# Moving the score-difference matmul from a three-bank to a four-bank PSUM ring in a two-attention, gated prompt kernel

## The chip, the cores and the metric

The kernel runs on one core of a Trainium2 chip. The metric is the device time of one execution in microseconds (us). A core has a matrix engine (PE, with its weight loads shown apart as PEld), a vector engine (DVE), a scalar engine (ACT), GpSimd (POOL) and an engine that here only issues DMAs (SP). Matmuls write into PSUM, which has eight banks of 128 partitions by 512 fp32 values. Every engine takes its own instructions in program order, and engines wait for one another through semaphores.

## The reference: what is computed

Two attention blocks read the same `x` (2048 tokens, 512 wide) with separate weights, each with 32 heads of width 16. Their results are mixed with a gate per token:

```python
q, k, v = split(x @ wqkv)                      # per block, 32 heads of 16
p = softmax(q @ k.T * 16 ** -0.5)              # full, 2048 x 2048 per head
a = (p @ v) @ wo                               # the same for b with its own weights
g = sigmoid((x * gate_w).sum(-1))
out = g * a + (1 - g) * b
```

The 64 heads (32 in each block) give 64 score matrices of 2048 by 2048.

## The kernel before: tiles, stages and order

**Stages.** A prologue (to about 300 us) projects `x` onto queries, keys and values and writes them to DRAM by head. The main stage (about 305 to 2841 us) goes through the 64 heads, 16 key tiles of 128 keys each. The last 75 us finish the last head and the output projection. Output projections of finished groups of heads (`project_out`, L449 to L464) also stand inside the main stage, 16 at about 1659 us and 16 at about 2644 us.

**Two sets of scores.** Softmax needs the maximum of each query's row ahead of the exponentials. So the scores are computed twice. Plain scores (a query tile of 128 rows against 512 keys, L135) are only reduced to a row maximum; they run 20 tiles ahead. Transposed scores (128 keys against 512 queries, L615) carry the maxima in two added rows, go through `exp` on ACT (L617) into the tile `p`, and `p` is multiplied with `v` into the bank `acc` (L576).

**Plain scores by differences.** A query tile needs the maximum over four blocks of 512 keys. On every second tile, blocks 0 and 1 are taken together: one matmul gives the score *differences* (`x_st` holds key block 1 minus key block 0; `max_rise`, L144), ACT takes their positive part, `relu` (L147), into a buffer `rise` in SBUF, and DVE adds that to the scores of block 0 and takes the maximum in one instruction (`max_pair`, L149 to L153). So one DVE pass covers two blocks.

**The round.** The loop at L626 takes two key tiles at a time; I call one pass a round. Its order is written out by hand in a string, read letter by letter (L640):

```python
    FULL = "m3memeem3meAe2Dmeee"
```

Here `m` is a plain score block with its DVE maximum (L145), `e` a transposed score block with its exp (L642), `D` the differences with their relu (L648), `A` the block that is added to them (L651), and a digit so many quarters of the product with `v` (L661). I number the letters: m1 to m6, e1 to e8. A round therefore issues on PE: m1, 3 quarters, m2, e1, m3, e2, e3, m4, 3 quarters, m5, e4, A, e5, 2 quarters, D, m6, e6, e7, e8. ACT has nine passes in a round (e1 to e5, D, e6 to e8), DVE seven (m1 to m5, A, m6). The pair A in a round uses the differences that D wrote in the round before.

**Two matmuls at a time.** Score matmuls use 48 or 50 of the array's 128 rows. `rows()` (L117) lets them alternate between the lower and the upper half, so that two neighbours can run side by side. Products with `v` use all rows, in four column groups.

**PSUM.** Three banks are the ring `ps_m` (L61), four the ring `ps_st` (L327), one is `acc`. A tile of a ring takes the banks in turn: with three banks a matmul waits until the engine that reads the tile three before it is done, with four banks the tile four before it. In the round, `ps_m` serves m1 to m6, A and D, eight tiles; `ps_st` serves e1 to e8. A `project_out` takes one more tile of `ps_m` (L445).

**Once a head** (every eighth round): ACT copies `acc` out (`ev`, L593) between e5 and D, DVE reduces the maxima (`mrow`, L161) at the end of a round and transposes them (`mt`, L168) in another.

Of the kernel before, what the change touches and what calls it, by code (L numbers as in the profile page):

```python
# [23 lines left out]
F32 = mybir.dt.float32  # L24
# [8 lines left out]
P = 128  # L33
# [18 lines left out]
def gated_mha(ctx: ExitStack, tc: tile.TileContext, xT, x, wqkv_a, wo_a, wqkv_b, wo_b, gate_w, out):  # L52
# [8 lines left out]
    ps_m = ctx.enter_context(tc.tile_pool(name="ps_m", bufs=3, space=PSUM))  # L61
# [55 lines left out]
    def rows():  # L117
        turn[0] ^= 1
        return HALVES[1 - turn[0]]

    def scores_bank(m, c):
        h, t = divmod(m, NT)
        if h not in mxp:
            mxp[h] = small.tile([P, NT, 4], F32, name="mxp")
            if h:
                pool.memset(mxp[h][:, FIRST % NT if h == 1 else 0::2, 1:2], LOWEST)
        ps = ps_m.tile([P, 512], F32, name="ps_m")
        b = rows()
        q = q_st[h % 3]
        if c == "rise":  # L130
            assert b == 0
            k = x_st[h % 2][:]
        else:
            k = k_st[h % 3][b:b + SC, c * 512:(c + 1) * 512]
        pe.matmul(ps, q[b:b + SC, t * P:(t + 1) * P], k, start=True, stop=True)  # L135
        return ps, mxp[h][:, t]

    def max_plain(m, c):
        ps, o = scores_bank(m, c)
        dve.tensor_reduce(o[:, c:c + 1], ps, op=ALU.max, axis=AX.X)  # L140
# [3 lines left out]
    def max_rise(m):  # L144
        ps, _ = scores_bank(m, "rise")  # L145
        rises[m] = small.tile([P, 512], F32, name="rise")
        act.activation(rises[m], ps, AF.Relu)  # L147

    def max_pair(m):  # L149
        ps, o = scores_bank(m, 0)  # L150
        rise = rises.pop(m)
        dve.tensor_tensor_reduce(out=rise, in0=ps, in1=rise, scale=1.0, scalar=LOWEST,  # L152
                                 op0=ALU.add, op1=ALU.max, accum_out=o[:, 0:1])  # L153
# [173 lines left out]
    ps_st = ctx.enter_context(tc.tile_pool(name="ps_st", bufs=4, space=PSUM))  # L327
# [369 lines left out]
```

## Time and profile before

| What | Value |
|---|---|
| Median of three runs | 2918.81 us (2918.76 to 2918.82) |
| The profiled execution, own time | 2918.34 us |
| Its span in the profile | 2916.6 us |
| Granted PE clock, mean | 0.998 |
| Relu passes of differences (L147) | 501 |
| exp passes (L617) | 4096 |

The span is what the profile covers; 1.7 us of the execution's own time lie around it. Busy time is the time in which an engine had at least one instruction running. The PE's busy time has modelled ends and says little about waits: where the PE waits, its matmuls in flight still count. The weight loads (PEld) show when the PE issued, and in brackets how long the weight path was idle and what ended that; a gap while a long product streams is no stall.

### The profile page before, as it was taken

How to read it: one execution, taken by the hardware profiler on the slowest of the kernel's cores; microseconds unless marked ns; L12 is line 12 of the kernel's file. 1: busy time of each engine (PE TensorE's matmuls, PEld its weight loads, DVE VectorE, ACT ScalarE, POOL GpSimd, SP SyncE). 2: the span in 40 equal slices, each digit the busy share in tenths (PEclk: the TensorE clock that was granted, in tenths of full speed). 3: DMA queues.
4: the chain of work that ended last, by engine and by line, in shares of the span. 5: the costliest groups of instructions: out<-in, count | busy, mean ns of one | idle time of the engine just before them, and what ended most of it. 6: DMA issues, size and time to landing. Idle time of an engine off the chain costs nothing.

```text
span 2916.6 us, 65382 instructions
## 1 busy us (share of the span) xinstructions
PE 2898.3 (99%) x26176; PEld 1417.1 (49%) x26176; DVE 2392.9 (82%) x4399; ACT 2497.8 (86%) x4758; POOL 255.0 (9%) x456
## 2 busy tenths in 40 slices
PE   8999999999999999999999999999999999999999
PEld 6877444444444444444444455444444444444544
DVE  4145899999899999999999877899999899998784
ACT  3221899999999999999999877899999999998785
POOL 1010112100000000000100231000000001011201
PEclk9999999999999999999999999999999999999999
DMA  7673333223333322333432342332223333233302
GB/s 258 193 255 129 78 70 77 60 53 55 67 60 57 57 57 46 54 57 56 86 56 52 93 103 54 56 58 49 58 50 57 56 75 67 52 70 87 70 13 90
DMA packets 91126, 225.25 MB, mean 77 GB/s; under 512 B 24150, under 2 KB 34358, under 8 KB 78278
## 3 DMA queue, kind: packets, MB, share of 16 engines
q1 hardware_dynamic: 88262, 212.15, 32.5%
q0 software_dynamic: 2560, 8.91, 1.2%
q8 instruction: 206, 3.38, 0.5%
q14 instruction: 98, 0.80, 0.1%
HBM read 152.07 MB, written 68.94 MB: 76 GB/s over the span
## 4 chain that ended last, share of the span: by engine, by line
PE 97%; DMA 1%; ACT 1%; DVE 0%; issue 0%; SPq 0%; DVEq 0%
PE ps_m L135 39%; PE acc L576 37%; PE ps_st L615 10%; PE ps_pro L232 5%; PE ps_m L458 3%; PE ps_pro L264 3%; ACT p L617 1%; DMA raw<-in_xT 0%; DMA k_st<-kd 0%; DMA qd<-part 0%; PE ps_st L458 0%; PE ps_st L509 0%; DVE mxp L140 0%; PE ps_m L509 0%; DVE part L237 0%
## 5 line engine op out<-in xcount | busy, mean ns | idle before, releaser
L617 ACT ACTIVATE p<-ps_st 128x512 f32<-128x512 f32 x4096 | 2153.7, 606 | 118.0 <-PE ps_st L615 84.5
L140 DVE TENSOR_REDUCE mxp<-ps_m 128x1 f32<-128x512 f32 x3094 | 1956.7, 684 | 261.1 <-PE ps_st L615 190.7
L135 PE MATMUL ps_m<-k_st,q_st 48*128 48x512 f32 x3595 | 1375.2, 453 | 0.9 <-DVE mxp L140 0.4
L576 PE MATMUL acc<-p,vg 128*17 128x384 f32 (+1 forms) x16368 | 1186.2, 384 | 2.9 <-ACT ev L584 2.0
L615 PE MATMUL ps_st<-q_st,k_st 50*128 50x512 f32 x4096 | 1187.4, 421 | 0.0
L135 PEld LDWEIGHTS ps_m<-k_st,q_st 48*128 48x128 f32 x3595 | 616.1, 184 | 690.3 <-ACT p L617 298.2
L615 PEld LDWEIGHTS ps_st<-q_st,k_st 50*128 50x128 f32 x4096 | 606.1, 185 | 45.8 <-ACT p L617 24.4
L576 PEld LDWEIGHTS acc<-p,vg 128*17 128x17 f32 x16368 | 314.8, 96 | 455.2 <-issue 435.6
L152 DVE CUSTOM_DVE_ANT_0 rise<-ps_m,rise 128x512 f32<-128x512 f32 x501 | 339.9, 678 | 0.0
L147 ACT ACTIVATE rise<-ps_m 128x512 f32<-128x512 f32 x501 | 301.5, 602 | 42.4 <-PE ps_m L135 0.3
L135 PE MATMUL ps_m<-x_st,q_st 48*128 48x512 f32 x501 | 249.4, 498 | 0.0
L162 POOL CAST mparts<-mrow 128x16 fp32r<-128x16 f32 x64 | 12.7, 198 | 2119.3 <-DVE mrow L161 2119.3
L135 PEld LDWEIGHTS ps_m<-x_st,q_st 48*128 48x128 f32 x501 | 91.7, 183 | 212.3 <-DVE mxp L140 183.8
L236 ACT CAST part<-ps_pro 128x1024 fp32r<-128x1024 f32 x32 | 32.5, 1015 | 134.8 <-PE ps_pro L232 113.3
L237 DVE TENSOR_TENSOR part<-ps_pro,part 128x1024 fp32r<-128x1024 f32 x32 | 39.2, 1224 | 101.1 <-ACT part L236 81.7
L458 PE MATMUL ps_m<-wo,ot 128*128 128x512 f32 (+1 forms) x354 | 90.7, 401 | 0.1
L267 ACT COPY v_st<-ps_pro 128x512 f32<-128x512 f32 x31 | 18.2, 587 | 77.8 <-PE ps_pro L264 74.6
L232 PE MATMUL ps_pro<-xh,whi 128*128 128x512 f32 x256 | 72.5, 402 | 9.6 <-ACT xh L218 9.1
L458 PEld LDWEIGHTS ps_m<-wo,ot 128*128 128x128 f32 (+1 forms) x354 | 64.0, 188 | 20.6 <-ACT rise L147 5.8
L232 PE MATMUL ps_pro<-xh,wlo 128*128 128x512 f32 x256 | 69.4, 393 | 0.0
L232 PE MATMUL ps_pro<-xl,whi 128*128 128x512 f32 x256 | 69.0, 391 | 0.0
L232 PEld LDWEIGHTS ps_pro<-xh,whi 128*128 128x128 f32 x256 | 47.3, 189 | 25.4 <-ACT xh L218 11.8
(99 smaller groups left out, 807.1 us busy)
## 6 DMA issues: line engine op xcount, KB each, us to landing
k_st<-kd SPq DMA_DIRECT2D x128, 256.0 KB
q_st<-qd SPq DMA_DIRECT2D x128, 256.0 KB
qd<-part SPq DMA_DIRECT2D x32, 512.0 KB
kd<-part SPq DMA_DIRECT2D x32, 512.0 KB
k_st<-kd SPq DMA_DIRECT2D x128, 128.0 KB
q_st<-qd SPq DMA_DIRECT2D x128, 128.0 KB
od<-ev SPq DMA_DIRECT2D x63, 256.0 KB
vd<-v_st SPq DMA_DIRECT2D x32, 272.0 KB
```

The source lines that it names most:

```text
L135: pe.matmul(ps, q[b:b + SC, t * P:(t + 1) * P], k, start=True, stop=True)
L140: dve.tensor_reduce(o[:, c:c + 1], ps, op=ALU.max, axis=AX.X)
L147: act.activation(rises[m], ps, AF.Relu)
L152: dve.tensor_tensor_reduce(out=rise, in0=ps, in1=rise, scale=1.0, scalar=LOWEST, op0=ALU.add, op1=ALU.max, accum_out=o[:, 0:1])
L232: pe.matmul(ps[:, c * 512:(c + 1) * 512], a[:, k], b[:, k], start=n == 0, stop=n == 3 * KC - 1)
L236: act.copy(pt[0], ps)
L237: dve.tensor_tensor(pt[1], ps, pt[0].bitcast(F32), op=ALU.subtract)
L264: pe.matmul(ps[:, :DM], a[:, k, o:o + P], b[:, k], start=n == 0, stop=n == 3 * KC - 1)
L458: pe.matmul(ps, ot[a][:n, slot, sl], wt[b][:n, g], start=G == groups[0] and i == 0, stop=G == groups[-1] and i == 2)
L576: pe.matmul(acc[32 * c:32 * c + 17, qa * P:qb * P], v[:, 4 * a + c if final else kt, j], p[:, c * 512 + qa * P:c * 512 + qb * P], start=fi ...
L615: pe.matmul(ps, k[b:b + SC + 2, kk * P:(kk + 1) * P], q[b:b + SC + 2, cc * 512:(cc + 1) * 512], start=True, stop=True)
L617: act.activation(pt[r][:, c * 512:(c + 1) * 512], ps, AF.Exp, scale=SCALE)
```

## The change

The matmul of the score differences takes its PSUM tile from the ring `ps_st` in place of `ps_m`. Relu then reads a bank of `ps_st`. Nothing else in the source changes; `ps_m` serves seven tiles a round and `ps_st` nine.

```diff
-        ps = ps_m.tile([P, 512], F32, name="ps_m")
+        pool_ = ps_st if c == "rise" else ps_m
+        ps = pool_.tile([P, 512], F32, name="ps_st" if c == "rise" else "ps_m")
         b = rows()
         q = q_st[h % 3]
         if c == "rise":
```

The line numbers after it are one higher than in the kernel before.

## The prediction

> **What bounds the kernel now.** I read the windows of the main stage first, then one round instruction by instruction, then the waits. The busy times in a window (PE, PEld, DVE, ACT, POOL; then the clock), and the same window with the difference matmuls alone:
>
> ```profile
> 1000.00:1200.00 200.00, 200.00 (x1970) 89.01 (x1966) 180.76 (x339) 194.36 (x375) 5.45 (x19) 1.00 0.30 57
> ```
>
> ```profile
> 1000.00:1200.00 200.00, 20.39 (x41) 1.00 0.30 57
> ```
>
> 41 rounds in 200 us make a round of 4.88 us. ACT looks full at 194 of 200 us, but its passes overlap, so busy time hides how much more it could do. The timeline of one round tells that; letters are those of the round's string (D is the matmul from `x_st`):
>
> ```profile
> 1016.60 0.68 DVE L140 TENSOR_REDUCE mxp<-ps_m 128x1 f32<-128x512 f32 x1
> ...
> 1017.16 0.49 PE L135 MATMUL ps_m<-x_st,q_st 48*128 48x512 f32 x1
> ...
> 1017.33 0.50 PE L135 MATMUL ps_m<-k_st,q_st 48*128 48x512 f32 x1
> ...
> 1017.80 0.08 DVE L152 DVE_READ_ACCUMULATOR2_ANT mxp<- 128x1 f32 x1
> 1017.86 1.30 DVE L140 TENSOR_REDUCE mxp<-ps_m 128x1 f32<-128x512 f32 x2
> 1017.93 0.18 PEld L135 LDWEIGHTS ps_m<-k_st,q_st 48*128 48x128 f32 x1 [0.25 <-DVE mxp L152]
> ...
> 1019.13 0.50 PE L135 MATMUL ps_m<-k_st,q_st 48*128 48x512 f32 x1
> ...
> 1019.67 2.48 DVE L140 TENSOR_REDUCE mxp<-ps_m 128x1 f32<-128x512 f32 x4 [0.50 <-PE ps_st L615]
> ...
> 1022.03 0.50 PE L135 MATMUL ps_m<-x_st,q_st 48*128 48x512 f32 x1
> ```
>
> D to D is 1022.03 - 1017.16 = 4.87 us. DVE stood idle 0.50 us before m2, so it isn't the bound. Two matmuls are late. m6 (1017.33) could run beside D but starts 0.17 later: it takes the bank of m5, whose maximum ends at 1016.60 + 0.68 = 1017.28; the PE goes on 0.05 later. m1 of the next round (1017.93) takes A's bank, and A's last DVE instruction ends at 1017.80 + 0.08 = 1017.88, again 0.05 before. So the PE waits for the three-bank ring, at a place where DVE is still working through m5, A and m6 one after the other. In the waits view (sum, times, longest):
>
> ```profile
> PEld ps_m L135 <- DVE mxp L152: 126.5, 490, 0.3
> ```
>
> That is m1's alone. What both waits cost is seen in a round of this same trace that began with empty rings, because the PE had just run at half clock and both readers had caught up:
>
> ```profile
> 313.54 0.50 PE L135 MATMUL ps_m<-x_st,q_st 48*128 48x512 f32 x1
> ...
> 313.54 0.49 PE L135 MATMUL ps_m<-k_st,q_st 48*128 48x512 f32 x1
> ...
> 313.88 0.63 PE L615 MATMUL ps_st<-q_st,k_st 50*128 50x512 f32 x3
> ...
> 314.07 0.60 ACT L147 ACTIVATE rise<-ps_m 128x512 f32<-128x512 f32 x1 [0.28 <-PE ps_m L135]
> ...
> 314.56 4.02 ACT L617 ACTIVATE p<-ps_st 128x512 f32<-128x512 f32 x8
> 315.21 0.18 PEld L135 LDWEIGHTS ps_m<-k_st,q_st 48*128 48x128 f32 x1 [0.64 <-ACT p L617]
> ...
> 315.70 0.18 PEld L615 LDWEIGHTS ps_st<-q_st,k_st 50*128 50x128 f32 x1 [0.19 <-ACT p L617]
> ...
> 318.12 0.50 PE L135 MATMUL ps_m<-x_st,q_st 48*128 48x512 f32 x1
> ```
>
> m6 starts with D, e8 ends at 314.51, and m2 is issued 315.21 - 313.54 = 1.67 after D, against 1019.13 - 1017.16 = 1.97 in the usual round: 0.30 us less. The 0.64 before m2 is named a wait, but it is there in this round too: while products with `v` stream, the weight path pauses. Such rows are no stalls. The whole free round took 318.12 - 313.54 = 4.58.
>
> **The change part by part.** No work is added or taken away; banks change hands. Following the rings letter by letter (the built program's waits agree), in `ps_m` three things change: m6 waits for m4's maximum in place of m5's, m1 for m5's in place of A's, m2 for A's in place of relu. m3, m4, m5 and A wait for what they waited for. In `ps_st`, D now waits for e2's exp, e6 for e3's, e7 for e4's, e8 for e5's, e1 for relu; e2 to e5 as before.
>
> *What goes.* m4's maximum starts (2.48 - 0.68)/3 = 0.60 before m5's and is over by about 1016.68, before D; m5's is over at 1017.28, and m1, behind e6 to e8, is due no earlier than the second pair of the free round, 313.88 - 313.54 = 0.34 after D, at 1017.50. Both waits end early enough, which is the free round's 0.30.
>
> *What is late next, DVE.* From m2's maximum to the end of m1's DVE has seven passes, 2.48 for the first four, then A, m6 and m1, and all seven take 4.36: m1's ends at 1017.86 + 1.30 = 1019.16, 0.51 before the next m2's. m4 needs m1's bank. It is issued together with e3, in the free round at 315.70, when m2's maximum could start 0.04 later (315.21 + 0.49 + 0.04); that issue cost 0.02. So with a round of 4.60 PE may go on 4.60 - 4.36 - 0.05 = 0.19 before m2's maximum and has to by 0.06 before it: 0.13 us of reserve and no wait.
>
> *What is late next, ACT.* Eight exps follow relu in 4.02 us, so passes end (4.02 - 0.60)/7 = 0.49 apart. Counted from D in the free round: relu ends at 1.13, e7 at 2.11, e8 at 2.60, e5 at 5.04. PE issues about 0.05 after an end, and a score matmul ends 0.50 after its issue (D's row: 0.49). e3 waits for e7, as before: 315.70 is 2.16, which costs 0.02 of the 4.58. The second half of the products needs e8 (2.65 against about 2.74): free. D, e6 and e7 need e2 to e4, over at 3.57, 4.06 and 4.55, before D comes at 4.58. e8 needs e5: issue at 5.09, end at 5.59, where the free round would end it at 4.58 + 314.51 - 313.54 = 5.55. So e8 is some 0.04 to 0.05 late, and m1 and the products stand behind it on PE. A longer round gives ACT more time, so about half of that remains, and it covers e3's 0.02: a round of 4.57 + 0.03 = **4.60**. ACT's own floor, nine passes at 0.49, is 4.41.
>
> *Once a head.* Relu in the round of `ev` comes late, and DVE has two passes more:
>
> ```profile
> 1012.27 0.49 PE L135 MATMUL ps_m<-x_st,q_st 48*128 48x512 f32 x1
> ...
> 1013.07 0.63 ACT L147 ACTIVATE rise<-ps_m 128x512 f32<-128x512 f32 x1
> ```
>
> ```profile
> L161 DVE TENSOR_REDUCE mrow<-mxp 128x16 f32<-128x64 f32 x64 | 14.1, 220 | 2.2
> L168 DVE STREAM_TRANSPOSE mt<-mparts 128x32 f32<-128x32 f32 x64 | 12.8, 201 | 0.6 <-POOL mparts L163 0.6
> ```
>
> Relu starts 0.80 after D in place of 0.53. Hidden before, since e3 had 0.3 us to spare; then e3 loses about 0.28. mrow and mt exceed DVE's reserve of 0.13 by 0.09 and 0.07 at most. Taken together some 0.45 per eight rounds, 0.06 a round: 4.66.
>
> *The relu's second wait.* In the built program relu now has an explicit wait for DVE (the `rise` buffer; the pair of the round before, long over) ahead of its wait for PE; the same kind of pair left e1, which had it before. Its price is between these: relu with one wait starts 314.07 - 314.04 = 0.03 after its matmul, and e1 with two waits at
>
> ```profile
> 1019.14 0.50 PE L615 MATMUL ps_st<-q_st,k_st 50*128 50x512 f32 x1
> ```
>
> ```profile
> 1019.76 0.60 ACT L617 ACTIVATE p<-ps_st 128x512 f32<-128x512 f32 x1
> ```
>
> 0.12 after. So it costs 0 to 0.09, and nothing below: a wait can't bring a pass forward. I take 0, because e1 also had an exp running ahead of it until 1019.76, and because relu's added wait comes first and is long fulfilled. The Trainium skill, page "Perfetto Trace Analysis", section "Identifying Dependency Chains", says that an instruction waiting for several engines may get separate semaphore instructions ahead of it. By that alone the upper end would hold, and it is the first rival below.
>
> *Sum.* 501 difference matmuls make 500 rounds; the rounds that hold an output projection have the same two waits. 500 x (4.88 - 4.66) = 110 us. Prologue, projections and the end don't change. The profiled execution took 2918.34 us (0.5 below the median of the runs, nothing against the range), so 2918.3 - 110 = **2808 us**.
>
> **The rivals.**
>
> *ACT sets the round.* If relu's second wait costs 0.09, e7 ends that much later, and e3 with it: 4.57 + 0.02 + 0.09 = 4.68, with the heads 4.74 to 4.75: 500 x 0.13 = 65 us, 2853. For it: e1's row. Against it: the order of relu's two waits. The time lies between 2830 and 2853.
>
> *PE alone sets the round.* If e8 and e3 aren't late and the heads cost nothing more, the full 0.30 goes: 2918 - 150 = 2768. For it: the free round. Against it: 315.70, where ACT held e3 already.
>
> *No change.* The waits on DVE are replaced by equal ones on ACT, or the rings don't turn as I count. It needs 0.30 us of new waits; ACT's nine passes end 0.49 apart and leave 4.88 - 4.41 = 0.47 a round. 2918.
>
> *Slower: the clock.* The PE ran at half clock once:
>
> ```profile
> 302.00:312.00 10.00, 9.61 (x47) 3.88 (x45) 7.64 (x13) 6.29 (x12) 1.88 (x2) 0.53 1.00 172
> ```
>
> If short waits for ACT between groups made it drop again, each such 10 us would lose about 5 us; 22 of them eat the gain, and 30 give 2808 + 150 = 2958. The Trainium skill, page "TensorE: Matmul & The Clock Gate", section "A second HAM failure mode: psum-queue depth-cycling", tells of PE short idles between groups that make the clock swing. Against it: the window at 1000 us has clock 1.00 with waits of 0.17 and 0.13 in every round, and those that I expect are shorter.
>
> **How the numbers follow.** Forecast (2785 to 2830) 0.62; ACT (2830 to 2853) 0.15; PE alone (2768 to 2785) 0.10; no change 0.04; slower 0.06; between 2853 and 2912, 0.03. The range is from the PE's end to ACT's, 2768 to 2853, and holds 0.87. Faster by over 0.2% (some 6 us, about what a measurement of this kernel can tell from no change): 0.90; within it 0.04; slower 0.06.
>
> **What would show it.** In the changed profile m6 starts with D, and the row of the weight path waiting for L153 (126.5 us before) all but goes. A row of weight loads of `ps_st` waiting for ACT grows, at e8 and in the `ev` rounds at e3. Windows at clock 1.00 hold 43 difference matmuls in 200 us in place of 41. Relu starts 0.03 after its matmul; if 0.12, the first rival holds. If 41 stay, the rings are not what I think; if m6 still starts 0.17 after D, the step on `ps_m` is wrong.

## The result, and the profile after

| | Before | After |
|---|---|---|
| Median | 2918.78 us (2918.71 to 2918.82, 4 runs) | 2804.91 us (2804.70 to 2806.24, 4 runs) |
| Span of the profiled execution | 2916.6 us | 2802.9 us |
| Granted PE clock, mean | 0.998 | 0.999 |

The ratio is 0.9611 (95% interval 0.9594 to 0.9627): 114 us faster. The forecast was 2808 us, 110 us faster, in a range of 2768 to 2853.

Where the time went is seen from the difference matmuls, one a round, in the view of one tile (operation, number, shortest, median and longest in ns, first and last start). Before:

```profile
L135 PEld LDWEIGHTS ps_m<-x_st,q_st x501: 182/183/285, 305.2 to 2835.7; 48*128 48x128 f32 x167
```

and after:

```profile
L136 PEld LDWEIGHTS ps_st<-x_st,q_st x501: 182/183/334, 304.3 to 2722.3; 48*128 48x128 f32 x167
```

The 500 rounds took 2530.5 us and now take 2418.0: 112.5 of the 114 us lie there, 0.225 a round. In a window of 200 us there are now 43 of them, and ACT and DVE are both fuller than before (first row; PE, PEld, DVE, ACT, POOL):

```profile
1000.00:1200.00 200.00, 200.00 (x2066) 85.40 (x2064) 187.02 (x356) 196.49 (x393) 5.92 (x22) 1.00 0.31 57
```

```profile
1000.00:1200.00 200.00, 21.35 (x43) 1.00 0.31 57
```

One usual round of the changed kernel, to be laid beside the round of the prediction:

```profile
1025.99 0.50 PE L136 MATMUL ps_st<-x_st,q_st 48*128 48x512 f32 x1
1025.99 0.18 PEld L136 LDWEIGHTS ps_m<-k_st,q_st 48*128 48x128 f32 x1
1025.99 0.50 PE L136 MATMUL ps_m<-k_st,q_st 48*128 48x512 f32 x1
...
1026.48 0.18 PEld L616 LDWEIGHTS ps_st<-q_st,k_st 50*128 50x128 f32 x1 [0.19 <-ACT p L618]
1026.48 0.18 PEld L136 LDWEIGHTS ps_m<-k_st,q_st 48*128 48x128 f32 x1
1026.52 0.60 ACT L148 ACTIVATE rise<-ps_st 128x512 f32<-128x512 f32 x1
1026.56 0.42 PE L136 MATMUL ps_m<-k_st,q_st 48*128 48x512 f32 x1
1026.63 0.08 DVE L153 DVE_READ_ACCUMULATOR2_ANT mxp<- 128x1 f32 x1
...
1027.68 0.49 PE L136 MATMUL ps_m<-k_st,q_st 48*128 48x512 f32 x1
...
1028.15 0.18 PEld L616 LDWEIGHTS ps_st<-q_st,k_st 50*128 50x128 f32 x1 [0.17 <-ACT p L618]
...
1028.20 2.48 DVE L141 TENSOR_REDUCE mxp<-ps_m 128x1 f32<-128x512 f32 x4 [0.29 <-PE ps_st L616]
...
1030.59 0.50 PE L136 MATMUL ps_st<-x_st,q_st 48*128 48x512 f32 x1
```

D and m6 start together (1025.99). m1's weights are issued at 1026.48, 0.15 before A's last DVE instruction begins (1026.63): it no longer depends on A. m2 comes 1.69 after D (1027.68), where it came 1.97 after. The round is 4.60. What now holds PE, for hundredths, is the ring of the transposed scores: e8's weights at 1026.48 and e3's at 1028.15, both released by ACT. In the waits view the row of m1's wait for A (126.5 us before) is gone, and the weight loads of the transposed scores wait longer for ACT; before and after:

```profile
PEld ps_st L615 <- ACT p L617: 24.4, 95, 0.4
```

```profile
PEld ps_st L616 <- ACT p L618: 179.4, 864, 0.4
```

### The profile page after: what moved, and what is told of

Its sections match the earlier page's. It is cut to its first block, busy times and chain, and to the rows that moved or that the text cites. A ratio compares the mean times of both kernels' runs of the same rounds, so it can differ in the third digit from the quotient of the medians.

```text
span 2802.9 us, 65443 instructions
## 1 busy us (share of the span) xinstructions
PE 2785.4 (99%) x26176; PEld 1319.3 (47%) x26176; DVE 2363.9 (84%) x4399; ACT 2419.9 (86%) x4758; POOL 254.8 (9%) x456
## 4 chain that ended last, share of the span: by engine, by line
PE 97%; DMA 1%; ACT 1%; DVE 1%; issue 0%; SPq 0%; DVEq 0%
PE acc L577 38%; PE ps_m L136 25%; PE ps_st L616 13%; PE ps_st L136 8%; PE ps_pro L233 5%; PE ps_m L459 3%; PE ps_pro L265 3%; ACT p L618 1%; DMA raw<-in_xT 0%; DMA k_st<-kd 0%; DMA qd<-part 0%; DVE mxp L141 0%; PE ps_st L459 0%; PE ps_st L510 0%; PE ps_m L510 0%
## 5 line engine op out<-in xcount | busy, mean ns | idle before, releaser
L618 ACT ACTIVATE p<-ps_st 128x512 f32<-128x512 f32 x4096 | 2077.0, 625 | 88.5 <-PE ps_st L616 73.8
L136 PE MATMUL ps_m<-k_st,q_st 48*128 48x512 f32 x3595 | 1359.7, 446 | 1.2 <-DVE mxp L141 0.4
L616 PE MATMUL ps_st<-q_st,k_st 50*128 50x512 f32 x4096 | 1218.1, 427 | 0.0
L616 PEld LDWEIGHTS ps_st<-q_st,k_st 50*128 50x128 f32 x4096 | 618.9, 185 | 198.6 <-ACT p L618 179.4
L148 ACT ACTIVATE rise<-ps_st 128x512 f32<-128x512 f32 x501 | 301.7, 602 | 36.6
L136 PE MATMUL ps_st<-x_st,q_st 48*128 48x512 f32 x501 | 249.1, 497 | 0.0
L136 PEld LDWEIGHTS ps_st<-x_st,q_st 48*128 48x128 f32 x501 | 91.8, 183 | 211.8 <-ACT p L618 211.4
```

Of the source, the lines that this page charges most:

```text
L616: pe.matmul(ps, k[b:b + SC + 2, kk * P:(kk + 1) * P], q[b:b + SC + 2, cc * 512:(cc + 1) * 512], start=True, stop=True)
L618: act.activation(pt[r][:, c * 512:(c + 1) * 512], ps, AF.Exp, scale=SCALE)
```

## The experiments

Eleven more kernels were run. Each ratio below is against the kernel before in the same job, whose median was 2918.4 to 2918.9 us.

**Which of the two waits held the round?** First m6's alone is taken away, in the kernel before, by its place in the string (e6 moves ahead of D too, so relu comes later on ACT):

```diff
-    FULL = "m3memeem3meAe2Dmeee"
+    FULL = "m3memeem3meAe2meDee"
```

> The rings of before; in the round's string the end reads 2meDee in place of 2Dmeee, so m6 takes its bank ahead of D, the bank of m4, and its wait for m5's maximum goes. m1 still waits for A's. My theory: m1's wait alone sets the start of the products, m6's lies behind it; the round stays at 4.87 and the time at 2919 us, within 6 us. Rival, each wait costs its own share: m6's 0.17 goes, 500 x 0.17 = 85 us, about 2834 us.

Measured: 2923.61 us, ratio 1.0016 (1.0007 to 1.0025). m6's wait is gone and nothing is gained; the 0.16% lost was not expected by either theory. Up to the first output projections its difference matmuls keep pace with those of the kernel before; the 5 us are lost from there on. The trace shows m1 at the same distance from A as before:

```profile
1017.18 0.08 DVE L152 DVE_READ_ACCUMULATOR2_ANT mxp<- 128x1 f32 x1
1017.18 1.36 DVE L140 TENSOR_REDUCE mxp<-ps_m 128x1 f32<-128x512 f32 x2
1017.32 0.18 PEld L135 LDWEIGHTS ps_m<-k_st,q_st 48*128 48x128 f32 x1 [0.27 <-DVE mxp L152]
```

A ends at 1017.26 and m1 is issued 0.06 later. A matmul that is ready earlier helps nothing if a later one in the same queue still waits.

Then each wait is put back alone into the changed kernel. The three plain banks are named and drawn from a list; the swapped tile takes the second oldest bank in place of the oldest, and the next tile the oldest:

```diff
+    ring = [0, 1, 2]
+
+    def bank_m(second=False):
+        ring.append(ring.pop(1 if second else 0))
+        return ps_m.tile([P, 512], F32, name=f"ps_m{ring[-1]}", bufs=1)
...
-                max_plain(*plain.pop(0))
+                max_plain(*plain.pop(0), second=len(plain) == 5)
```

This is m1's; for m6's the number is 0.

> The changed kernel, with one wait put back: m1 takes the bank of A (as before the change) and m2 that of m5; m6 keeps m4's. My theory: from m2's maximum to A's last instruction DVE needs 3.09 us, then m1 is issued 0.05 later, ends 0.50 after, and m2's next maximum comes 1.24 later, so a round is 4.88 and the whole gain is lost: 2918 us. Rival, each wait costs its own share: m1's 0.13 comes back, about 2870 us. Second rival, the gain came from D not waiting in the plain ring at all: the time stays at 2805 us.

Measured: 2917.84 us, ratio 0.9998 (0.9989 to 1.0008). One wait, of m1 for A, gives the whole gain back, although D is still in the four-bank ring. A round of it:

```profile
1016.76 0.50 PE L141 MATMUL ps_st<-x_st,q_st 48*128 48x512 f32 x1
1016.76 0.50 PE L141 MATMUL ps_m<-k_st,q_st 48*128 48x512 f32 x1
...
1017.41 0.08 DVE L158 DVE_READ_ACCUMULATOR2_ANT mxp<- 128x1 f32 x1
...
1017.54 0.50 PE L141 MATMUL ps_m<-k_st,q_st 48*128 48x512 f32 x1
...
1021.63 0.50 PE L141 MATMUL ps_st<-x_st,q_st 48*128 48x512 f32 x1
```

D and m6 run side by side, m1 starts 0.05 after A's end (1017.49), and D to D is 4.87.

> The changed kernel with the other wait put back: m6 takes m5's bank, m1 that of m4; m2 to A as in the changed kernel. My theory: m6 is 0.17 late, e7 and m1 stand behind it in the same half of the array, so m1 ends at 1.14 after D in place of 0.97; that hides the lateness of e8 and half of that of e3: a round of 4.74 to 4.76, 2918 - 500 x 0.12 = 2858 us. Rival, m6's wait is worth nothing without m1's: 2805 us. Second rival, it adds to the new waits in full: 4.66 + 0.17, about 2890 us.

Measured: 2852.15 us, ratio 0.9771 (0.9755 to 0.9787): 47 us of the gain lost, 6 us from what I expected and far from both rivals (2805 and 2890). Both kernels draw named banks, so the naming by itself can't be what cost 113 us in the first; in this one m6 is issued 0.17 after D, as was put back. So the two waits overlap: m1's is worth 113 us by itself, m6's 47 us where m1's is gone and nothing where it isn't.

**Is it D in the ring of ACT, or four banks for the plain scores?** The kernel before with one bank moved:

```diff
-    ps_m = ctx.enter_context(tc.tile_pool(name="ps_m", bufs=3, space=PSUM))
+    ps_m = ctx.enter_context(tc.tile_pool(name="ps_m", bufs=4, space=PSUM))
...
-    ps_st = ctx.enter_context(tc.tile_pool(name="ps_st", bufs=4, space=PSUM))
+    ps_st = ctx.enter_context(tc.tile_pool(name="ps_st", bufs=3, space=PSUM))
```

> The kernel before, with the fourth bank moved: four banks for the plain scores (D stays there, eight tiles), three for the transposed ones. The plain ring then makes m6 wait for m4 and m1 for m5, as in the changed kernel, but e2 waits for e7 and e3 for e8. My theory: e8's exp ends 2.60 after D, e3's matmul may begin at 2.76 where it is due at 2.24, so a round is 4.57 + 0.51 = 5.08 and with the ev rounds 5.10: 2918 + 500 x 0.22 = about 3025 us. Rival, the gain of the change is only that the plain scores have more banks for their tiles: 2805 us or less.

Measured: 3019.24 us, ratio 1.0345 (1.0330 to 1.0360), slower. The plain ring has no wait left at m6, but e2 and e3 are late:

```profile
1018.07 0.18 PEld L615 LDWEIGHTS ps_st<-q_st,k_st 50*128 50x128 f32 x1 [0.19 <-ACT p L617]
...
1018.56 0.18 PEld L615 LDWEIGHTS ps_st<-q_st,k_st 50*128 50x128 f32 x1 [0.31 <-ACT p L617]
```

e3 is issued 0.98 after m2 (1017.58 to 1018.56) where the free round has 0.49 (315.21 to 315.70). What counts is which reader's end each tile waits for, not how many banks a ring has.

**Does ACT hold the new round, and did it hold the old one?** Exps over 384 of 512 columns, in both kernels. So that no unwritten memory is read, the three `p` buffers are allocated once and filled with ones; that step alone is the control.

```diff
+    p_tiles = [ppool.tile([P, S], F32, name=f"p{i}", bufs=1) for i in range(3)]
+    for t in p_tiles:
+        pool.memset(t, 1.0)
...
-            pt[r] = ppool.tile([P, S], F32, name="p")
+            pt[r] = p_tiles[r % 3]
...
-        act.activation(pt[r][:, c * 512:(c + 1) * 512], ps, AF.Exp, scale=SCALE)
+        act.activation(pt[r][:, c * 512:c * 512 + 384], ps[:, :384], AF.Exp, scale=SCALE)
```

> Control for the next two: the changed kernel with its three p buffers allocated once and filled once, in place of a rotating pool. Nothing else differs. Every theory: 2805 us, within 6 us.

> The changed kernel with fixed p buffers, and every exp over 384 of its 512 columns (the exps of the last 128 queries of each block of 512 are left out, p holds ones there). Passes would end some 0.37 to 0.40 us apart (in proportion to the 0.49). My theory: a round of the changed kernel is held by ACT, e8 waiting for e5 by about 0.03 and e3 for e7 by 0.28 in the ev rounds. With shorter exps e8 is free and e3 loses about 0.1 in the ev rounds, DVE's share of the heads stays: a mean round of 4.60 to 4.61 in place of 4.65, about 2780 us. Rival, ACT holds nothing any more and the PE's own stream is the bound: 2805 us.

> The kernel before with the same shorter exps (the same part left out). My theory: before the change the round is held by A's maximum through m1, and ACT, although busy 97% of the main stage, holds nothing: 2919 us, within 6 us. Rival, ACT was the bound before: nine passes, eight of them some 0.1 us shorter, would take the round down to the PE's 4.57 to 4.60: 2770 to 2785 us.

Measured: control 2830.31 us (ratio 0.9695, 0.9681 to 0.9710), changed kernel with short exps 2766.57 us (0.9479, 0.9463 to 0.9495), kernel before with short exps 2918.75 us (1.0001, 0.9992 to 1.0010).

The last is the clearest: shorter exps give the kernel before nothing. In its window ACT's busy time fell from 194 to 160 of 200 us, and the rate stayed at 41 rounds:

```profile
1000.00:1200.00 200.00, 200.00 (x1968) 89.42 (x1968) 180.59 (x340) 160.32 (x375) 5.91 (x22) 1.00 0.30 57
```

The kernel before with fixed buffers alone was not run, but a gain and a loss that cancel don't fit its trace with short exps: ACT is idle ahead of relu in most rounds (0.26 us at 1020.23), and m1 is still issued 0.06 after A's end:

```profile
1020.34 0.08 DVE L152 DVE_READ_ACCUMULATOR2_ANT mxp<- 128x1 f32 x1
...
1020.48 0.18 PEld L135 LDWEIGHTS ps_m<-k_st,q_st 48*128 48x128 f32 x1 [0.26 <-DVE mxp L152]
```

In the changed kernel they gain 64 us over the control and 38 us over the changed kernel itself, where I had expected 25. The rounds with `ev`, 4.88 in the changed kernel, take 4.57 like the usual ones, and waits of the transposed scores' weight loads for ACT all but vanish. The group of these loads in the control, then with short exps (busy, mean | idle before, released by):

```profile
L619 PEld LDWEIGHTS ps_st<-q_st,k_st 50*128 50x128 f32 x4096 | 619.0, 184 | 207.8 <-ACT p L621 159.9 <-issue 3.4
```

```profile
L619 PEld LDWEIGHTS ps_st<-q_st,k_st 50*128 50x128 f32 x4096 | 619.0, 185 | 62.3 <-issue 15.7 <-ACT p L621 4.2
```

2767 us is where the prediction put a round set by PE alone (2768).

The control failed my expectation by 25 us. Its trace has 512 event instructions at the exps' line, one a round, where the changed kernel has one in all. They wait for PE; the exp behind each, e4 in the round below, then has a second wait, for ACT itself, which I take to be for an earlier write of the fixed buffer. e4's matmul and its exp:

```profile
1020.79 0.50 PE L619 MATMUL ps_st<-q_st,k_st 50*128 50x512 f32 x1
```

```profile
1021.42 0.60 ACT L621 ACTIVATE p<-ps_st 128x512 f32<-128x512 f32 x1
```

The exp starts 0.13 after its matmul's end. That fits a chain through e5 to e8 and longer rounds, but it was read from the trace and not tried by itself.

**What lengthens one round of every eight, beside `ev`?** I had put it down to DVE's two extra passes. First `mrow` is issued one DVE instruction later, where DVE is idle, in both kernels:

```diff
-            max_split(m // NT)
+            split.append(m // NT)
...
                 max_plain(*plain.pop(0))
+                if split:
+                    max_split(split.pop())
```

> The changed kernel; the reduction of a head's maxima (mrow, 0.22 us on DVE) is issued one DVE instruction later, behind m1 of the next round in place of ahead of it. My theory: DVE stands idle between m1 and m2, so there it costs nothing, while ahead of m1 it makes m4 wait for m1's bank. The lengthened round (4.81 in place of 4.60 in the changed kernel's profile) goes: 0.19 x 63 = 12 us, 2793 us. Rival, the lengthened round is not mrow's doing, or the delay comes back at another place: 2805 us.

> The kernel before with the same step of mrow. My theory: there DVE has 0.5 us of idle time behind m1 and m4 comes later, so mrow ahead of m1 cost nothing: 2919 us, within 4 us. Rival, mrow costs the same in both: 2907 us.

Measured: 2803.98 us (ratio 0.9606, 0.9593 to 0.9619) and 2917.89 us (0.9998, 0.9989 to 1.0007). Neither differs from its base by what can be told apart; the long round stays, and my theory about `mrow` falls as it stood. In the changed kernel's trace m1 of such a round shows two event instructions ahead of it on PE, because it is the first to read newly loaded stacks. So the loads were left out:

```diff
-        if kt == 0 and h + 2 < NH:
+        if kt == 0 and h == 0:
```

> The changed kernel without the loads of heads 3 to 63 (they compute with the stacks of heads 0 to 2; the loads are left out, all else stays). In every eighth round of the changed kernel m1 is the first to read a head's newly loaded stacks and waits for four DMAs, and mrow stands in the same round; that round is 4.81 in place of 4.60. Theory A: two event instructions ahead of m1 on PE, 0.13 us apart, make it late; without the loads the round is 4.60 and the time 63 x 0.2 = 12 us less, about 2793 us. Theory B: the lengthening comes from DVE's two passes more a head (mrow and mt), which stay: 2805 us.

> The kernel before without the loads of heads 3 to 63 (left out as in the other run). There m1 waits for A's maximum in any case, and the same events cost only what goes beyond that wait: every eighth round is 4.94 to 4.97 in place of 4.88. Theory A: 63 x 0.07 = 4 us less, about 2914 us. Theory B: 2919 us.

Measured: 2799.03 us (ratio 0.9590, 0.9577 to 0.9603) and 2918.55 us (1.0000, 0.9991 to 1.0009). In the changed kernel the long round was 1007.30 - 1002.49 = 4.81:

```profile
1002.49 0.50 PE L136 MATMUL ps_st<-x_st,q_st 48*128 48x512 f32 x1
...
1007.30 0.49 PE L136 MATMUL ps_st<-x_st,q_st 48*128 48x512 f32 x1
```

and without the loads it is 4.66:

```profile
1000.49 0.50 PE L136 MATMUL ps_st<-x_st,q_st 48*128 48x512 f32 x1
...
1005.15 0.49 PE L136 MATMUL ps_st<-x_st,q_st 48*128 48x512 f32 x1
```

Most such rounds take 4.78 with the loads and 4.66 without. The times alone hardly show it, since the two intervals of the ratio overlap; but between the first and the last difference matmul the trace has 2410.6 us in place of 2418.0.

So the loads make about 0.12 of the 0.18 by which that round is longer. Their traffic doesn't: from 990 to 1006 us the DMA share of the changed kernel is 0.00, and the round is as long as the others of its kind. What differs is m1, issued 0.72 after D behind the event instructions (first row), and 0.50 after D without the loads (second):

```profile
1003.21 0.18 PEld L136 LDWEIGHTS ps_m<-k_st,q_st 48*128 48x128 f32 x1
```

```profile
1000.99 0.18 PEld L136 LDWEIGHTS ps_m<-k_st,q_st 48*128 48x128 f32 x1
```

The 0.06 that stays fits `mrow` after all. Without the loads m4 is issued 0.08 after e3, where in a usual round they go together, and 0.05 after the end of m1's maximum, which runs on DVE behind `mrow`:

```profile
1001.86 0.22 DVE L162 TENSOR_REDUCE mrow<-mxp 128x16 f32<-128x64 f32 x1
...
1002.65 0.18 PEld L616 LDWEIGHTS ps_st<-q_st,k_st 50*128 50x128 f32 x1 [0.16 <-ACT p L618]
1002.73 0.18 PEld L136 LDWEIGHTS ps_m<-k_st,q_st 48*128 48x128 f32 x1
```

With the loads the PE is later than that in any case, so moving `mrow` alone gains nothing. No run moves `mrow` with the loads left out, so its share is read from the trace and not tried. The kernel before gains nothing from either step, against my 4 us: its own lengthened round, 4.97 once a head, is still there.

## Why the prediction was right, point by point

- *The bound.* Right. The kernel before was held by m1's wait for A's maximum; putting that one wait back costs all of the gain (2917.84 us), and relieving ACT gains nothing (2918.75 us). What the prediction says of DVE, "it isn't the bound", is true of its busy share only: from m2's maximum to A's end, 3.09 of the 4.88 us are DVE's passes, and m1's wait ties the round to them. Where `mt` stands among them (at 1001.88) that stretch takes 3.18 and the round 4.97.
- *0.30 us a round go.* Right: D to m2 fell from 1.97 to 1.69. The prediction described m6's 0.17 and m1's wait as two waits that make 0.30 together. The runs show more: m6's lay wholly behind m1's.
- *e8 waits for e5 next, a round of 4.60.* Right: 4.60, with e8 released by ACT in the round above. With shorter exps e8's weights come 0.35 after D in place of 0.49, the usual round takes 4.57 and the kernel 2767 us.
- *Relu's second wait costs nothing.* Right: in the round above relu starts at 1026.52, 0.03 after its matmul's end at 1026.49. The Trainium skill's rule on separate event instructions (page "Perfetto Trace Analysis", section "Identifying Dependency Chains") agrees with the trace: 499 of them stand at relu's line, where the kernel before has 501 at the exps' line and none at relu's. The one ahead of this relu runs at 1025.6, so it was over in time.
- *`ev`, 0.28 in one round of eight.* Right. The round of `ev` that begins at 1016.49 shows relu late behind it and e3 waiting for ACT:

```profile
1016.49 0.49 PE L136 MATMUL ps_st<-x_st,q_st 48*128 48x512 f32 x1
...
1016.81 0.60 ACT L594 COPY ev<-acc 128x512 f32<-128x512 f32 x1
...
1017.27 0.64 ACT L148 ACTIVATE rise<-ps_st 128x512 f32<-128x512 f32 x1
...
1018.95 0.18 PEld L616 LDWEIGHTS ps_st<-q_st,k_st 50*128 50x128 f32 x1 [0.31 <-ACT p L618]
```

  D is at 1016.49, relu 0.78 after it, and e3's weights 2.46 after it in place of 2.16 in the usual round above.
- *mrow and mt, 0.16 in one round of eight.* The size came near (0.18 in the trace), but partly by luck, since the cause was wrong in the main: leaving out the loads takes 0.12 of it. `mrow` makes m4 late as the prediction has it, by 0.08 where 0.09 at most was forecast, but this shows only without the loads; behind `mt` (1004.53 there) no matmul is seen late. The step that failed is the reading of a lengthened round by the DVE passes that stand in it, without a look at what else PE waits for there.
- *The sum.* 110 us forecast, 114 measured. 112.5 of them lie between the first and the last difference matmul, as the sum had it.
- *The slower rival, the clock.* It didn't happen: the windows stay at 1.00.

## What to carry to other kernels

A ring of banks makes each tile wait for a particular earlier tile, the one as many places back as the ring has banks; write down for each matmul which reader's end that is, because moving one tile to another ring shifts all the pairs behind it. Look for the wait that ends last ahead of the next long block on the in-order engine; earlier waits hide behind it, so that taking one of them away alone gains nothing, as with m6 and with `mrow` here. Engines at 90% and more busy may hold nothing. A round in the same trace that starts with empty buffers shows what the waits are worth ahead of any change.

## What the runs showed of the hardware that I had not expected

- A fixed buffer in place of a rotating one cost 25 us with the same work (2830.31 against 2804.91 us), where its exp, with a wait for PE ahead of a second wait, starts 0.13 us after its matmul and not 0.03 as relu with the two waits the other way round. That this makes the 25 us was not tried by itself.
- The first reader of newly loaded tiles pays on PE although the data are long there (the DMA share is 0.00 from 990 to 1006 us). The changed kernel's plain-score line around such an m1:

```profile
L136 PEldq EVENT_SEMAPHORE  x3: 51/51/51, 1003.0 to 1003.3; - x3
```

  Three event instructions of 51 ns stand around m1 in 0.3 us. Without the loads there are none at that place, and such a round is some 0.12 shorter (4.78 to 4.66 in most).
